# First feed-forward product of five chunks from seven quarter products, with shared buffers

## Chip, cores and metric

The kernel runs on one core of a Trainium2 chip. The metric is device time in microseconds; the median of several runs is compared.

## What is computed

Two layers, each of sliding, dilated attention followed by a dense feed-forward part, both with a layer norm ahead and a residual. The change touches the feed-forward part.

```
B, S, D, F = 1, 2048, 576, 4608      # x [1,2048,576] f32; w1 [576,4608], w2 [4608,576] f32
H, W, dil = 32, 8, 2                 # attention: 32 heads of 18, 8 keys at distance 0,2,..,14

def _A_ref(x, wqkv, wo):             # q,k,v = x@wqkv; softmax over the 8 keys; o @ wo
    ...
def _B_ref(x, w1, w2):
    h = jnp.einsum("bsd,df->bsf", x, w1)
    h = _silu(h)
    return jnp.einsum("bsf,fd->bsd", h, w2)

x = A_x
x = x + _A_ref(_layernorm(x), A_wqkv, A_wo)
x = x + _B_ref(_layernorm(x), B_w1, B_w2)
x = x + _A_ref(_layernorm(x), A_wqkv, A_wo)
x = x + _B_ref(_layernorm(x), B_w1, B_w2)
```

## The kernel before

The 2048 rows are cut into four chunks of 512 (NC = 4, four tiles j of 128 rows), and each of the two layers goes through them, so there are eight stages s = 0 to 7. Every product is made in three passes of f16: an operand is split into a high half and a low half, and high x high, high x low and low x high are summed in PSUM. In a contraction of 576 (four blocks of 128 and one of 64) that is 14 matmuls: `passes` (L333) yields them, the block of 64 holding its high rows and low rows one above the other.

`front(s)` loads the chunk (`load_x`), makes a layer norm whose f16 halves are transposed by DMA on SP's queue (`layer_norm`, `transposed`, L361), makes q, k and v in four units u of eight heads (L564), computes attention on VectorE (L661 to L702), projects with `wo` (`project`, L733) and makes the layer norm for the feed-forward part, whose transposed result XT[s] lies in a buffer `xb`. For the first layer the q, k, v of all chunks are made at the start and lie in DRAM. From s = 4 on, `load_wq` (L510) loads the prepared weights of each unit.

`ffn(s)` works over 36 blocks f of 128 columns of w1. For each: one product z of 14 matmuls with 512 moving columns (L858) into a PSUM bank `z`; ScalarE makes SiLU (L860, tile `hs`) and the high half of h (L862); VectorE makes the low half (L865). Blocks form groups (6 in stage 0, otherwise G1 = 9). For each group and tile j the second product accumulates 6 matmuls per block, 288 columns each (L876), into `acc`, and VectorE adds it to x with the group's scale (L740). In stage 0 the f32 weights are loaded, scaled by powers of two and split (`raw_load`, `raw_split`) and the f16 halves are stored to DRAM (`w1s`, `w2s`); later stages load them from there on SP's queue (L745, L750). The chunk's x goes to DRAM or to the output at the end.

The order of the instructions isn't that of the code. `Plan` collects operations with an engine, a duration, a priority (smaller goes first) and the tiles they read and write; `Plan.order` plays them through, engine by engine, gives each buffer a slot when its first operation starts, and issues the operations in the order so found. So each engine's order, SP's and POOL's DMA queues included, is fixed ahead by these durations. Priorities are tied to the stage: `front(s)` has s - 1, the products of `ffn(s)` s + 0.5, and its loads, ScalarE and VectorE work s - 0.5. A buffer `tag` has its own slots: 2 banks of PSUM for `z`, 2 for `misc` (q, k, v and small sums), 2 x 2 for `acc`; in SBUF for instance 1 `xa` and 2 `xb` (transposed inputs), 2 `wq`, 2 `kv`, 6 `w1`, 11 `w2`, 10 `h`, 3 `hs`.

Of the kernel before, what the change touches and what calls it, by code (L numbers as in the profile page):

```python
# [16 lines left out]
P = 128  # L17
D = 576
# [16 lines left out]
G1 = 9  # L35
LNS = 1024.0
# [14 lines left out]
class Plan:  # L51
# [10 lines left out]
    def slots(self, tag, tiles, turns):  # L62

        self.tags[tag] = tiles
        self.turns[tag] = 0 if turns else None
        self.named[tag] = 0
# [35 lines left out]
    def order(self):  # L102
        free = {t: list(range(len(x))) for t, x in self.tags.items()}
# [63 lines left out]
        while done < len(self.ops):  # L167
# [9 lines left out]
            while events and events[0][0] <= now:  # L177
                _, _, b = heapq.heappop(events)
                free[b.tag].append(b.slot)
            for e in engines:  # L180
# [7 lines left out]
                while ready[e]:  # L188
# [5 lines left out]
                    if all(len(free[t]) - want.get(t, 0) >= c for t, c in n.items()) and all(  # L194
                            self.turns[b.tag] in (None, b.turn) for b in need):
                        o = x[2]
                        break
# [7 lines left out]
                for b in o.bufs:  # L205
                    if b.slot is None:
                        b.slot = free[b.tag].pop(0)
# [24 lines left out]
def sliding_attention_silu_ffn(ctx: ExitStack, tc: tile.TileContext, x, wqkv, wo, w1, w2, out):  # L232
# [17 lines left out]

    tag("x", 8, [P, D], F32)
    tag("xa", 1, [P, 9, TB], F16)
    tag("xb", 2, [P, 9, TB], F16)
    tag("wq", 2, [P, 10, 3 * UC], F16)
    tag("kv", 2, [P, NI, 2, UC], F32)
    tag("qt", 2, [P, NJ, UC], F32)
    tag("o", 1, [P, NJ, D], F32)
    tag("lg", 1, [P, NJ, W, UH], F32)
    tag("pe", 2, [P, NJ, W, UH], F32)
    tag("pr", 1, [P, 2, W, UC], F32)  # L260
    tag("mx", 2, [P, NJ, UH], F32, turns=False)
    tag("y", 2, [P, D], F32, turns=False)
# [3 lines left out]
    tag("w1", 6, [P, 10, P], F16)  # L266
    tag("w2", 11, [P, 2, D], F16)
    tag("h", 10, [P, 2, TB], F16)
    tag("hs", 3, [P, TB], F32)
# [3 lines left out]
    tag("z", 2, [P, TB], F32, ps)  # L273
    tag("acc", 2, [P, 2, 512], F32, ps, turns=False)
    tag("misc", 2, [P, 512], F32, ps, turns=False)
# [3 lines left out]
    w2s = [tc.dram_tile([P, 2 * D], F16, name=f"w2s{f}") for f in range(NFT)]  # L279
    wqs = [tc.dram_tile([P, 30 * UC], F16, name=f"wqs{u}") for u in range(NU)]  # L280
# [35 lines left out]
    shs = [cp.tile([P, NFT], F32, name=f"sh{i}") for i in range(2)]  # L316
    d2s = [cp.tile([P, NFT], F32, name=f"d2{i}") for i in range(2)]
# [30 lines left out]
    def transposed(src, dst, key, j, prio, on_pe=False):  # L348


        if on_pe:
# [6 lines left out]
            op("PE", 0.8, turn, [(src, 0), (src, 1)], [m], prio)  # L358
# [8 lines left out]
    gate = []  # L367
    marks = []

    def layer_norm(xs, prio, into, on_act, on_pe=False):  # L370

        st, mv, nt, xT = Buf("st"), Buf("mv"), Buf("nt"), Buf(into)

# [42 lines left out]
        op("DVE", 2.6, newton, [(st, j) for j in range(NJ)] + [(mv, j) for j in range(NJ) if on_act < 2], [nt], prio)  # L416
        for j in range(NJ):
# [18 lines left out]
            else:  # L436
                op("DVE", 0.6, norm, [xs[j], (mv, j), nt], [y, (xT, "hold")], prio)
# [8 lines left out]
    class Unit:  # L446
# [6 lines left out]

        def __call__(self, k):
            if self.kind == "h":
                return T(self.bufs[k % 5])[:, k // 5, 0:QR]
            return T(self.bufs[0])[:, k, 0:QR]

    def raw_wq(u):

        rs = [Buf("h" if u < 2 else "w2") for _ in range(5)]
# [36 lines left out]
    def store_wq(u, w, m):  # L498
        def store():
# [4 lines left out]
            else:  # L504
                nc.gpsimd.dma_start(wqs[u].rearrange("p (k c) -> p k c", c=QR), T(w.bufs[0])[:, :, 0:QR])
        op("POOL", 2.8 if w.kind == "h" else 0.6, store, w.keys, [("wqs", u)], -0.6, nbytes=P * 20 * QR, after=marks[m:m + 1])

    def load_wq(u, prio):
        w = Unit("wq")
        op("SP", 0.4, lambda: nc.sync.dma_start(fl(T(w.bufs[0])), wqs[u]), [("wqs", u)], w.keys, prio, nbytes=P * 20 * QR)  # L510
        return w
# [83 lines left out]
    def attention(s, xT, wq, more=None):  # L595
# [4 lines left out]
        for u in range(NU):  # L600
# [10 lines left out]
            else:  # L611
                w = wq(u)
                if blk == 0:
# [3 lines left out]
                    op("POOL", 1.6, clear, [], [(kv, "edge")], pr_)  # L617
                else:
# [5 lines left out]
                    op("SP", 0.8, edge, [("eds", lay, par, u)], [(kv, "edge")], pr_, nbytes=20000)  # L624
                for j in range(NJ):
                    m = Buf("misc")

                    def evac(j=j, m=m, u=u, kv=kv, qt=qt):
# [5 lines left out]
                       [(xT, j)] + w.keys, [m], pr_)  # L634
# [52 lines left out]
            for j in range(0, NJ, 2):  # L687
# [15 lines left out]
                op("DVE", 2.63, tree, [], [(pr, 0), (pr, 1), (o, j, u), (o, j + 1, u)], pr_)  # L703
# [51 lines left out]
    def raw_load(f, prio):  # L755
# [15 lines left out]
        op("POOL", 0.6, lambda: nc.gpsimd.dma_start(fl(T(b).bitcast(F32)), w2[f * P:(f + 1) * P, :]), [], [b], prio,  # L771
           nbytes=P * 5 * D, after=late)

    def raw_split(f0, prio):
# [9 lines left out]
        def rb(f):  # L784
            return fl(T(raws[f][1]).bitcast(F32))
# [32 lines left out]
    def group_scale(i, g, n):  # L818

        sl = slice(g * n, (g + 1) * n)  # L820
        sh, d2 = shs[i], d2s[i]
# [6 lines left out]
        op("DVE", 0.7, fn, [("s12", f) for f in range(g * n, (g + 1) * n)], [("sh", i, g), ("cg", g)], -0.5)  # L828

    def ffn(s, xT, xs):  # L830
        raw = s == 0
        n, i = (G0, 0) if raw else (G1, 1)
        pp, pd = s + 0.5, s - 0.5
        lay, c = divmod(s, NC)
        for g in range(NFT // n):
            hb, wbs = [], []
            if raw:
# [5 lines left out]
                group_scale(0, g, n)  # L843
            for f in range(g * n, (g + 1) * n):
# [127 lines left out]
```

## Time and profile before

| | |
|---|---|
| Time, median of 3 runs | 2243.82 us (2238.85 to 2246.42) |
| Span of the profiled execution | 2240.2 us (its own time is not listed apart) |
| TensorE (PE) busy | 2181.8 us, 97% |
| VectorE (DVE) busy | 1396.7 us, 62% |
| ScalarE (ACT) busy | 740.3 us, 33% |
| GpSimd (POOL) busy | 201.4 us, 9% |
| First product L858 | 4032 matmuls, 887.4 us |
| Second product L876 | 6912 matmuls, 855.1 us |
| DMA | 334.54 MB, mean 149 GB/s |

PE is TensorE's matmuls and PEld its weight loads, which overlap them; SPq is the queue from which SP issues DMAs. The listed length of one matmul runs from its issue to its modelled end, so the rate is read from a run of matmuls: length divided by count. In a list of groups the numbers behind the bar are busy us and mean ns of one, then idle us ahead of it and what ended that. The clock is a share of TensorE's full clock; the DMA share is the mean busy share of the core's 16 DMA engines.

### The profile page before, as it was taken

What the parts mean: (1) busy time and instruction counts of PE and PEld (TensorE: products, weight loads), DVE (VectorE), ACT (ScalarE), POOL (GpSimd) and SP (SyncE); (2) the same over time, 40 slices, a digit from 0 to 9 for tenths busy, and PEclk for the clock granted to TensorE, in tenths of its full rate; (3) what the DMA queues carried; (4) which work ended last, traced back from release to release, by engine and by line L of the source; (5) the groups of instructions that cost most, each with busy time, mean ns of one, the idle gap of its engine ahead of it and who ended that gap; (6) DMA issues with size and microseconds to landing.
All of it is one profiled execution on the core that took longest, in us unless ns stands there. A gap on an engine that the chain in (4) does not pass through costs nothing.

```text
span 2240.2 us, 33794 instructions
## 1 busy us (share of the span) xinstructions
PE 2181.8 (97%) x13786; PEld 1349.1 (60%) x13786; DVE 1396.7 (62%) x2074; ACT 740.3 (33%) x1207; POOL 201.4 (9%) x329
## 2 busy tenths in 40 slices
PE   6999998989999999999999999999999999999998
PEld 3446565646766766655666656666666566666665
DVE  8898888979899511259833597346971389511111
ACT  7245675633223122233212232222322223222222
POOL 2123464400001000000000000000000000000000
PEclk9999999999999999999999999999999999999999
DMA  7677676675464433455444454454454643333331
GB/s 199 162 208 257 211 246 202 207 238 175 133 195 149 113 113 104 141 146 171 112 115 153 112 177 117 125 161 123 137 134 119 168 137 119 90 121 121 116 103 40
DMA packets 230148, 334.54 MB, mean 149 GB/s; under 512 B 116696, under 2 KB 136772, under 8 KB 226024
## 3 DMA queue, kind: packets, MB, share of 16 engines
q1 hardware_dynamic: 201024, 225.09, 35.4%
q0 software_dynamic: 19232, 63.86, 8.3%
q10 hardware_dynamic: 9736, 43.42, 6.2%
q8 instruction: 108, 1.77, 0.3%
q14 instruction: 48, 0.39, 0.1%
HBM read 240.08 MB, written 47.03 MB: 128 GB/s over the span
## 4 chain that ended last, share of the span: by engine, by line
issue 44%; PE 42%; DVE 7%; DMA 4%; POOL 1%; ACT 1%; ACTq 0%; POOLq 0%; SPq 0%; DVEq 0%
PE z L858 17%; PE acc L876 17%; PE z L564 3%; PE acc L733 3%; PE misc L564 2%; DVE pr L694 2%; DVE pr L701 1%; DVE lg L665 1%; DVE pr L661 1%; DMA w1s<-w 1%; DMA w<-in_B_w_dram 1%; DMA xb<-yh 0%; DMA w<-w2s 0%; DMA x<-in_A_x_dram 0%; DVE w L804 0%
## 5 line engine op out<-in xcount | busy, mean ns | idle before, releaser
L858 PE MATMUL z<-xb,w 128*128 128x512 f16 x4032 | 887.4, 380 | 19.8 <-ACT hs L860 15.7
L876 PE MATMUL acc<-w,h 128*128 128x288 f16 x6912 | 855.1, 286 | 0.0
L876 PEld LDWEIGHTS <-h 128*128 128x128 f16 x6912 | 676.3, 98 | 177.3
L858 PEld LDWEIGHTS <-w 128*128 128x128 f16 x4032 | 395.5, 98 | 489.4 <-issue 21.9
L860 ACT ACTIVATE hs<-z,d 128x512 f32<-128x512 f32 x288 | 197.4, 685 | 961.3 <-PE z L858 949.9
L865 DVE SCALAR_TENSOR_TENSOR h<-hs,sh,h 128x512 f16<-128x512 f32 x288 | 213.8, 748 | 317.3 <-ACT h L862 317.0
L740 DVE SCALAR_TENSOR_TENSOR x<-acc,d,x 128x576 f32<-128x576 f32 x136 | 110.9, 815 | 321.5 <-PE acc L876 321.3
L661 DVE TENSOR_TENSOR pr<-qt,kv 128x2304 f32<-128x2304 f32 x64 | 163.4, 2553 | 86.6 <-DMA kv<-kv 42.7
L862 ACT ACTIVATE h<-hs,sh 128x512 f16<-128x512 f32 x288 | 207.2, 721 | 9.0
L564 PEld LDWEIGHTS <-xa 128*128 128x128 f16 x1344 | 132.1, 99 | 117.0 <-issue 6.0
L564 PE MATMUL misc<-wq,xa 128*128 128x432 f16 x1008 | 189.4, 349 | 0.7 <-ACT qt L632 0.7
L694 DVE TENSOR_TENSOR pr<-kv,pe 128x1152 f32<-128x1152 f32 x128 | 169.4, 1352 | 1.3
L665 DVE TENSOR_REDUCE lg<-pr 128x128 f32<-128x2304 f32 x64 | 163.2, 2550 | 1.3
L701 DVE TENSOR_TENSOR pr<-pr 128x1152 f32<-128x1152 f32 (+1 forms) x128 | 135.3, 1057 | 3.5
L733 PE MATMUL acc<-wo,oT 128*128 128x288 f16 x896 | 114.5, 289 | 2.9 <-ACT oT L359 2.9
L733 PEld LDWEIGHTS <-oT 128*128 128x128 f16 x896 | 88.3, 99 | 28.7 <-ACT oT L359 3.0
L891 POOL DMA_DIRECT2D out_dram<-x x16 | 8.7, 544 | 910.3 <-DVE x L740 910.3
L630 ACT ACTIVATE kv<-misc,du 128x288 f32<-128x288 f32 x80 | 39.9, 499 | 142.2 <-PE misc L564 73.3
L564 PEld LDWEIGHTS <-xb 128*128 128x128 f16 x448 | 44.8, 100 | 49.1 <-issue 7.7
L684 ACT ACTIVATE pe<-lg 128x256 f32<-128x256 f32 x32 | 13.3, 415 | 167.8 <-DVE lg L675 160.5
L383 DVE BATCH_NORM_STATS2 st<-x 128x6 f32<-128x288 f32 x128 | 51.9, 448 | 10.3 <-DMA x<-xd 6.5
L564 PE MATMUL z<-wq,xb 128*128 128x432 f16 x224 | 43.3, 355 | 5.1 <-DMA xb<-yh 5.1
(118 smaller groups left out, 1094.5 us busy)
## 6 DMA issues: line engine op xcount, KB each, us to landing
w<-w1s SPq DMA_DIRECT2D x252, 320.0 KB
w<-w2s SPq DMA_DIRECT2D x252, 288.0 KB
kv<-kd ACTq DMA_DIRECT2D x12, 1584.0 KB
wq<-wqs SPq DMA_DIRECT2D x17, 1080.0 KB
w1s<-w POOLq DMA_DIRECT2D x36, 320.0 KB, 4.2
w<-in_B_w_dram POOLq DMA_DIRECT2D x36, 288.0 KB, 4.4
w2s<-w POOLq DMA_DIRECT2D x36, 288.0 KB, 4.3
kv<-kv ACTq DMA_DIRECT2D x20, 504.0 KB
```

What stands on the lines that cost most here:

```text
L564: nc.tensor.matmul(T(m)[:, :3 * UC], a, b, start=n == 0, stop=n == len(pl) - 1)
L661: nc.vector.tensor_tensor(T(pr), T(qt)[:, j:j + 2, None, :].to_broadcast([P, 2, W, UC]), win(T(kv), j, 2), op=ALU.mult)
L665: nc.vector.tensor_reduce(T(lg)[:, j:j + 2].rearrange("p a w h -> p (a w h)"), T(pr).rearrange("p a w (h d) -> p (a w h) d", d=DH), axis=A ...
L694: nc.vector.tensor_tensor(T(pr)[:, a].rearrange("p w (h d) -> p w h d", d=DH), v, T(pe)[:, j + a, :, :, None].to_broadcast([P, W, UH, DH]) ...
L701: nc.vector.tensor_tensor(t[:, :, 0:h, :], t[:, :, 0:h, :], t[:, :, h:2 * h, :], op=ALU.add)
L733: nc.tensor.matmul(T(acc)[:, h, 0:288], a, b[:, h * 288:(h + 1) * 288], start=n == 0, stop=n == len(pl) - 1)
L740: nc.vector.scalar_tensor_tensor(t, T(acc)[:, :, 0:288], d, t, op0=ALU.mult, op1=ALU.add)
L858: nc.tensor.matmul(T(z), v, u, start=m == 0, stop=m == len(pl) - 1)
L860: op("ACT", 0.7, lambda z=z, hs=hs, f=f: nc.scalar.activation(T(hs), T(z), AF.Silu, scale=d1[:, f:f + 1]), [z, ("s12", f)], [hs], pd, tabl ...
L862: op("ACT", 0.72, lambda hs=hs, h=h, f=f: nc.scalar.activation(T(h)[:, 0, :], T(hs), AF.Copy, scale=shs[i][:, f:f + 1]), [hs, ("sh", i, g) ...
L865: op("DVE", 0.75, lambda hs=hs, h=h, f=f: nc.vector.scalar_tensor_tensor(T(h)[:, 1, :], T(hs), shs[i][:, f:f + 1], T(h)[:, 0, :], op0=ALU. ...
L876: nc.tensor.matmul(T(acc)[:, h, 0:288], T(hb[q])[:, a, j * P:(j + 1) * P], T(wbs[q][0])[:, w, h * 288:(h + 1) * 288], start=q == 0 and m = ...
```

## The change

**Seven products.** In stages 3 to 7 (SF = 3) two blocks f, a pair p, are made together. The tokens are cut into halves of 256 (HT), the contraction into halves of 288 (HD), the pair into its two blocks: a 2 x 2 by 2 x 2 product. It is made by a scheme with seven products of sums and differences in place of eight. Each product is 7 matmuls with 256 moving columns (three blocks high x high, the third with 96 rows that also hold one crossed part, two low x high and two high x low). Sums that the scheme needs after the products are made partly by accumulating in a PSUM bank that has already been read, partly by ScalarE copies (`keep`) and VectorE additions (`add`).

**Prepared operands.** The layer norm of these stages (`into == "xt"`) makes seven sums of quarters per tile pair, their halves, and 70 transposed blocks per chunk (35 per pass, four DMA transposes for each of two passes) in place of 36 in four. The sums of w1's quarters are made once by `prepare`, 54 pieces (18 pairs times three row blocks): load from w1 by POOL's queue, four subtractions and the low half on VectorE, the high half on ScalarE, and a store to `wts` in DRAM. They have priority 1.2 and may start when stage 0 has all scales. The first 24 use buffer `pw`, the others take turns through `pw`, `pk` and `po`. `load_wt` then loads a pair's 35 blocks into four `w1` slots.

**Groups and buffers.** Groups have 6 blocks in all stages; in stages 3 to 7 the second product is issued one block at a time (STEP) with a priority 0.2 behind the first (LATE). Slots are now w1 8, w2 10, h 8, hs 4, y 1. `Plan` learns of slots that share memory: `xl` (q, k, v input of stages 4 to 7), `x0` to `x2`, the two `xt`, one of the two `wq` and `pw` overlap in one piece of SBUF; `pk` and `po` lie in `kv`, `o` and `pr`, and so do the layer norm's `ys` and `yS`; `zz` covers the four banks of `z` and `misc`. The layer norm, `load_wq` and the edge of keys of stages 4 to 7 wait for the transposes of the stage before, and `load_wq` also for the last four pieces of `prepare`. In the set-up the raw wqkv units change between `h` and `w2` buffers.

```diff
-G1 = 9
-LNS = 1024.0
+G1 = 6
+NP = NFT // 2
+HT = TB // 2
+HD = D // 2
+SF = 3
+PREP = 1.2
+STEP = 1
+LATE = 0.2
+EARLY = 24
+LNS = 512.0
...
+    shared("rb", 3 * XW + QW, [
+        ("wq", [("ra", 0, QW), (3 * XW, 3 * XW + QW)], cut(10), True),
+        ("xa", [(XW * i, XW * (i + 1)) for i in range(3)], cut(9), True),
+        ("xl", [(0, XW), (35 * HT, 35 * HT + XW)], cut(9), True),
...
+        ("xt", [(0, 35 * HT), (35 * HT, 70 * HT)], cut(35), True),
+        ("pw", [("ra", 0, 30 * P), (3 * XW, 3 * XW + 30 * P), (XW, XW + 30 * P)], lambda v: v, True)])
...
+    for t, at, turns in (("z", (0, 1), True), ("misc", (2, 3), False), ("zz", (0, 1, 2, 3), False)):
...
+        op("POOL", 1.2 if k < 2 else 2.4, load, [], [(r, 0)], prio, nbytes=P * 4 * P * 6, after=after)
...
+            nc.vector.tensor_tensor(v[:, 4], v[:, 7], v[:, 0], op=ALU.subtract)
+            nc.vector.tensor_tensor(v[:, 3], v[:, 5], v[:, 7], op=ALU.subtract)
+            nc.vector.tensor_tensor(v[:, 2], v[:, 5], v[:, 4], op=ALU.subtract)
+            nc.vector.tensor_tensor(v[:, 6], v[:, 1], v[:, 2], op=ALU.subtract)
...
+            d = wts[p].rearrange("p (a b c) -> p a b c", a=7, b=5)
+            nc.gpsimd.dma_start(d[:, :, k, :], cut_(0))
+            if k < 2:
+                nc.gpsimd.dma_start(d[:, :, 3 + k, :], cut_(1))
...
+        def product(z, c, m, first):
+            def mm():
+                pl = [(k, k) for k in range(3)] + [(k + 3, k) for k in range(2)] + [(k, k + 3) for k in range(2)]
+                for n, (i, j) in enumerate(pl):
+                    q = 96 if i == j == 2 else P
+                    nc.tensor.matmul(T(z)[:, 0:HT], T(w[m // 2])[0:q, m % 2 * 5 + j, :], T(xT)[0:q, 5 * c + i, :],
+                                     start=first and n == 0, stop=n == len(pl) - 1, skip_group_check=True)
+            op("PE", 0.78, mm, [(xT, 0), (xT, 1), w[m // 2]], [z], pp)
+
+        def keep(z, t, s, k):
+            op("ACT", 0.42, lambda: nc.scalar.activation(T(t)[:, s], T(z)[:, 0:HT], AF.Copy), [z], [(t, k)], pd - 0.2)
+
+        def add(z, t, s, k):
+            op("DVE", 0.43, lambda: nc.vector.tensor_tensor(T(t)[:, s], T(z)[:, 0:HT], T(t)[:, s], op=ALU.add),
+               [z], [(t, k)], pd - 0.2)
...
+        product(Y, 0, 0, True)
+        product(X, 1, 1, True)
+        keep(Y, b, lo, 0)
+        product(Y, 4, 2, False)
+        add(X, b, lo, 0)
+        product(V, 5, 3, True)
+        keep(Y, b, hi, 1)
+        product(Y, 3, 4, False)
+        keep(Y, a, hi, 1)
+        product(Y, 6, 5, False)
+        add(V, a, hi, 1)
+        product(V, 2, 6, False)
+        add(V, b, hi, 1)
+        silu(a, lo, [0], 0.42, Y)
+        silu(a, hi, [1], 0.42)
+        silu(b, slice(0, TB), [0, 1], 0.7)
...
-                step = n if n < 6 else 3
+                step = 3 if s < SF else STEP
...
+        if s == SF:
+            for i in range(3 * NP):
+                t = ("pw", "pk", "po")[(i + i // 3) % 3 if i >= EARLY else 0]
+                prepare(i // 3, i % 3, t, PREP, scaled + {"pw": [], "pk": read[-1:], "po": turned[-2:]}[t])
         ffn(s, XT[s], X[s])
```

More of the change, by code (lines that the diff above doesn't have):

```diff
@@ L102, in order, with spare, hold, fits @@
     def order(self):
-        free = {t: list(range(len(x))) for t, x in self.tags.items()}
+        alias, where = {}, {}
+        for t, us in self.units.items():
+            for i, u in enumerate(us):
+                for x in u:
+                    where.setdefault(x, []).append((t, i))
+        for t, us in self.units.items():
+            for i, u in enumerate(us):
+                alias[t, i] = sorted({k for x in u for k in where[x]})
+        kept = dict.fromkeys(alias, 0)
+        left_at = dict.fromkeys(alias, 0)
+        def spare(t):
+            return [i for i in range(len(self.units[t])) if not kept[t, i]]
+        def hold(t, i, by):
+            for k in alias[t, i]:
+                kept[k] += by
+        def fits(n, want):
+            taken = []
+            ok = True
+            for t, c in n.items():
+                left = spare(t)
+                if len(left) - want.get(t, 0) < c:
+                    ok = False
+                    break
+                if len(n) > 1:
+                    for i in left[:c]:
+                        hold(t, i, 1)
+                        taken.append((t, i))
+            for t, i in taken:
+                hold(t, i, -1)
+            return ok
         engines = sorted({o.eng for o in self.ops})
@@ L178, in order @@
                 _, _, b = heapq.heappop(events)
-                free[b.tag].append(b.slot)
+                hold(b.tag, b.slot, -1)
+                for k in alias[b.tag, b.slot]:
+                    left_at[k] = seq
             for e in engines:
@@ L193, in order @@
                         n[b.tag] = n.get(b.tag, 0) + 1
-                    if all(len(free[t]) - want.get(t, 0) >= c for t, c in n.items()) and all(
-                            self.turns[b.tag] in (None, b.turn) for b in need):
+                    if fits(n, want) and all(self.turns[b.tag] in (None, b.turn) for b in need):
                         o = x[2]
@@ L367, in sliding_attention_silu_ffn, with layer_norm @@
     gate = []
+    turned, scaled, read = [], [], []
     marks = []
-    def layer_norm(xs, prio, into, on_act, on_pe=False):
+    def layer_norm(xs, prio, into, on_act, on_pe=False, late=()):
         st, mv, nt, xT = Buf("st"), Buf("mv"), Buf("nt"), Buf(into)
+        view = lambda: T(xT)
         def total(j, i):
@@ L436, in layer_norm @@
             else:
-                op("DVE", 0.6, norm, [xs[j], (mv, j), nt], [y, (xT, "hold")], prio)
+                op("DVE", 0.6, norm, [xs[j], (mv, j), nt], [y, (xT, "hold")], prio,
+                   after=late)
                 o = op("DVE", 1.2, halves, [y], [(yh, 0), (yh, 1)], prio)
@@ new lines, in load_wt, with load, halves @@
+    def load_wt(p, prio):
+        ws = [Buf("w1") for _ in range(4)]
+        for i, w in enumerate(ws):
+            n = 10 if i < 3 else 5
+            def load(i=i, w=w, n=n):
+                nc.sync.dma_start(fl(T(w))[:, 0:n * P], wts[p][:, 10 * i * P:(10 * i + n) * P])
+            op("SP", 0.5, load, [("wts", p, k) for k in range(3)], [w], prio, nbytes=P * 2 * n * P)
+        return ws
+    def halves(f, hs, h, key, pd):
+        op("ACT", 0.72, lambda: nc.scalar.activation(T(h)[:, 0, :], T(hs), AF.Copy, scale=sh[:, f:f + 1]),
+           [(hs, 0), (hs, 1), key], [(h, 0)], pd)
+        op("DVE", 0.75, lambda: nc.vector.scalar_tensor_tensor(
+            T(h)[:, 1, :], T(hs), sh[:, f:f + 1], T(h)[:, 0, :], op0=ALU.mult, op1=ALU.subtract),
+           [(hs, 0), (hs, 1), (h, 0), key], [(h, 1)], pd)
```

217 lines of the change are left out of this document (165 added, 52 removed).

## The prediction

> **What bounds the kernel now.** I read the page first (busy shares and slices), then busy time by stage, then the chain of waits.
>
> ```profile
> PE 2181.8 (97%) x13786; PEld 1349.1 (60%) x13786; DVE 1396.7 (62%) x2074; ACT 740.3 (33%) x1207; POOL 201.4 (9%) x329
> PE   6999998989999999999999999999999999999998
> DVE  8898888979899511259833597346971389511111
> ...
> 0.00:488.00 488.00, 437.45 (x2670) 261.07 (x2671) 420.51 (x740) 278.90 (x514) 167.10 (x277) 0.98 0.69 217
> 488.00:716.00 228.00, 226.45 (x1462) 143.56 (x1462) 206.30 (x235) 72.16 (x94) 4.02 (x6) 0.99 0.50 159
> 716.00:944.00 228.00, 228.00 (x1480) 144.63 (x1479) 71.63 (x126) 50.70 (x72) 3.94 (x6) 1.00 0.40 120
> 944.00:1213.00 269.00, 269.00 (x1705) 166.64 (x1704) 166.09 (x234) 72.08 (x114) 11.52 (x17) 1.00 0.49 138
> 1751.70:2021.00 269.30, 269.30 (x1706) 166.74 (x1705) 162.21 (x224) 71.85 (x114) 2.19 (x5) 1.00 0.46 128
> ```
>
> The windows are my stages: set-up with chunk 0, then chunk 1, chunk 2, chunk 3 (with the attention of chunk 4), and the sixth chunk; their columns are PE, PEld, DVE, ACT and POOL busy, then clock, DMA share, GB/s. From 500 us on TensorE never idles and its clock is 1.00. So each chunk after the first lasts as long as its matmuls, and the change, which touches chunks 3 to 7, is priced on TensorE. VectorE is the other thing to watch: 206 of 228 us in chunk 1, but 72 of 228 in chunk 2.
>
> **The gain: the products.** From the chain in order of time (start, length, what, count), and a short stretch with small matmuls:
>
> ```profile
> 660.38 27.20 PE z L858 x126
> 687.58 26.46 PE acc L876 x216
> 966.55 25.55 PE misc L564 x140
> ...
> 218.59 1.17 PE L357 MATMUL acc<-ident,yh 128*128 128x128 f16 x18
> ...
> L876 PEld LDWEIGHTS <-h 128*128 128x128 f16 x6912 | 676.3, 98 | 177.3
> L357 PE MATMUL acc<-ident,yh x108: 217/219/314, 13.0 to 222.6; 128*128 128x128 f16 x108
> ```
>
> A matmul of 512 columns takes 27.20/126 = 0.2159 us, of 432 columns 25.55/140 = 0.1825, of 288 columns 26.46/216 = 0.1225. The line through these is 0.4167 ns a column and 2.5 ns fixed, so 256 columns cost 0.1092 us (estimate). Every matmul has its own weight load, listed at 98 ns; could that be a floor? The 18 transposes of 128 columns, each with its own load, take 1.17 us to the end of the last; less its 0.219 us, 0.95/17 = 0.056 us each. No floor as high as 0.109.
>
> For two column blocks f the kernel now issues 2 x 14 matmuls of 512: 6.04 us. The change issues 7 products x 7 matmuls of 256: 49 x 0.1092 = 5.35 us (the matmuls on 96 rows stream the same columns). That saves 0.69 us a pair, 18 pairs and 5 chunks: 62.2 us. The second product (L876) keeps its 864 matmuls a chunk.
>
> The Trainium skill, "TensorE: Matmul & The Clock Gate", section "Back-to-back issue gap", speaks against this: in a stream of weight loads and matmuls it gives about 81 ns a matmul at 128 columns and 131 at 512, so about 98 at 256 by a straight line (an estimate from that page). By that, a pair would go from 28 x 0.131 = 3.7 us to 49 x 0.098 = 4.8 us, and the kernel would lose some 100 us. The trace disagrees at both ends (0.056 and 0.2159 us), and its measured line decides.
>
> **What it adds on ScalarE and VectorE.** The nearest rows:
>
> ```profile
> L860 ACT ACTIVATE hs<-z,d 128x512 f32<-128x512 f32 x288 | 197.4, 685 | 961.3 <-PE z L858 949.9 <-DMA kv<-kv 3.2 <-DVE lg L665 3.1
> L630 ACT ACTIVATE kv<-misc,du 128x288 f32<-128x288 f32 x80 | 39.9, 499 | 142.2 <-PE misc L564 73.3 <-DVE pr L694 56.1 <-issue 9.1
> L632 ACT ACTIVATE qt<-misc,du 128x144 f32<-128x144 f32 x80 | 29.9, 374 | 0.0
> L684 ACT ACTIVATE pe<-lg 128x256 f32<-128x256 f32 x32 | 13.3, 415 | 167.8 <-DVE lg L675 160.5 <-DMA kv<-kv 7.2
> L675 DVE TENSOR_TENSOR lg<-lg,mx 128x256 f32<-128x256 f32 x32 | 13.6, 425 | 1.1
> L740 DVE SCALAR_TENSOR_TENSOR x<-acc,d,x 128x576 f32<-128x576 f32 x136 | 110.9, 815 | 321.5 <-PE acc L876 321.3
> L804 DVE SCALAR_TENSOR_TENSOR w<-w,s,w 128x640 f16<-128x640 f32 x36 | 31.7, 880 | 8.4 <-ACT w L802 8.4
> L802 ACT ACTIVATE w<-w,s 128x640 f16<-128x640 f32 x36 | 29.5, 819 | 21.1 <-DMA w1s<-w 10.7 <-PE z L858 9.6 <-DVE s L330 0.4
> L661 DVE TENSOR_TENSOR pr<-qt,kv 128x2304 f32<-128x2304 f32 x64 | 163.4, 2553 | 86.6 <-DMA kv<-kv 42.7 <-ACT kv L630 21.7 <-ACT qt L632 21.2
> L702 DVE TENSOR_TENSOR o<-pr 128x288 f32<-128x288 f32 x64 | 29.3, 458 | 2.6
> ```
>
> Per pair ScalarE gets three copies out of PSUM of 256 columns (0.47 us each, between L632 and L630) and its SiLU in three pieces (0.47, 0.42, 0.69) in place of two of 0.69: +1.6 us, 29 us a chunk, on an engine that is busy 72 of 269. VectorE gets three adds of 256 (0.425): 23 us a chunk; 24 in place of 16 adds into x (groups of 6): 6.5 us; the wider layer norm about 3 us. So 166 + 32 = 198 busy us in a chunk of 257. Both hide beside TensorE as long as order allows.
>
> The weight preparation is 54 pieces, from the end of chunk 0 on. Each: four subtractions of 128 columns (0.29 us, by the slope from L675 to L702) and one low half of 896 columns (1.16, slope of L740 and L804) on VectorE, 2.33 us; 1.03 us on ScalarE. That is 126 us of VectorE, 56 of ScalarE. VectorE had 456 - 278 = 178 us idle in chunks 1 and 2; groups of 6 take 13 and the norm 3. So 126 of 162 us fits before chunk 3, mostly in chunk 2. If that cover is gone, the rest falls into chunk 3 (59 us idle there).
>
> **What is late next: the front of chunk 4.** Its weight loads (L510) are made to wait for the last pieces and for the transposes of chunk 3; on SP's queue feed-forward weight loads stand behind them.
>
> ```profile
> 979.36 7.99 SPq L510 DMA_DIRECT2D wq<-wqs  x2
> ...
> 1135.95 7.71 SPq L361 DMA_TRANSPOSE xb<-yh  x4
> ...
> 1940.60 9.98 SPq L361 DMA_TRANSPOSE xb<-yh  x4
> ...
> L361 SPq DMA_TRANSPOSE xb<-yh x36: 1242/1300/4112, 30.7 to 1949.3; - x36
> ```
>
> Today the front of chunk 4 ends about 1146 and is needed at 1213: 67 us spare (the sixth chunk's: 1951 against 2021). After: 12 less from the shorter chunk, about 25 more VectorE work ahead of it, and four more transposes of 1.3 us each with their landing, some 8 us. Spare 20 us, provided the pieces end by about 979, where those loads go today. I take 5 us of stall at this boundary, between 0 (ends in time) and 59 (all of chunk 3's idle VectorE time used up by pieces ahead of it).
>
> **DMA.** Two windows calibrate: one with weight loads alone, one with transposes in small packets.
>
> ```profile
> DMA packets 3004, 6.48 MB, mean 116 GB/s; under 512 B 332, under 2 KB 332, under 8 KB 3002
> q1 hardware_dynamic: 3002, 6.45, 36.9%
> ...
> DMA packets 4881, 1.52 MB, mean 102 GB/s; under 512 B 4752, under 2 KB 4752, under 8 KB 4880
> q1 hardware_dynamic: 4880, 1.51, 49.3%
> ```
>
> The first (56 us, 2072 to 2128) moves 6.45 MB at 36.9%, so 312 GB/s when full; the second (15 us, 1940 to 1955) 1.51 MB at 49.3%: 204 GB/s. A pair's weights grow from 20 to 35 blocks of 32 KB, 0.66 to 1.15 MB: 8.8 MB a chunk, 28 us of full DMA; the 70 transposed blocks in place of the window's 36 some 7 us more. The share of chunks 3 to 6 rises from 0.49 to about 0.65; I cost it at nothing, since two pairs of weight buffers cover 11 us a pair. The prepared weights go out as 256-byte pieces, 18 x 1.15 = 20.6 MB: at 204 GB/s 101 us, and 54 x 0.26 = 14.2 MB of f32 quarters come in, 45 us: 146 us on top of a half-idle DMA over the 350 us from about 600 on. POOL issues these 234 transfers and is all but idle then (4 us per chunk). The Trainium skill, "DMA: Bandwidth & Descriptors", section "Specifications", says that pieces under 512 bytes lose line rate to read-modify-write; the second window agrees in direction (204 against 312 GB/s).
>
> **Waits within a pair.** Seven products share three banks; Y is read twice, and product 4, 3 and 6 each wait for a read; V's second product waits for a VectorE add. Between them the planner puts pieces of the second product (0.73 us, now one block at a time). The planner counts 0.42 us for the copies that I put at 0.47, so I take 2 x 0.05 = 0.1 us a pair, 9 us for 90 pairs. Below: nothing, as TensorE shows none now. Above: 3.4 us for a pair in an attention stretch (rival A).
>
> **Nothing on the path:** the smaller h, y and w2 buffer counts meet a first stage held by VectorE (420 of 488 us); I allow 8 us either way there.
>
> **Sum.** 2240.2 span - 62.2 + 9 + 5 = 2192. The page gives no time of its own for the profiled execution; the span lies 3.6 us under the median of 2243.8, so 2195.6; I say 2195.
>
> **Rivals.**
> A, slower: VectorE holds the products. While attention runs, its order is filled with operations of 2.55 us (L661). An add that arrives behind one waits 1.28 us on average, then takes 0.43; two per pair sit before a product (the bank of X, the second half of V): 3.4 us if nothing covers. About 110 us of VectorE-saturated time per chunk 3 to 6 is 8 pairs, 32 in all: 109 us in place of the 9 of the sum: 2195 - 9 + 109 = 2295. It decides once the mean wait over all 90 pairs passes 0.69 us. Against it: 24 free pieces of the second product per 21 products. Chance 0.13.
>
> B, part of the gain lost to the preparation: small stores and the gate on chunk 4's front run late, 20 to 40 us of stall near 1200: 2210 to 2237. For it: spare of only 20 us by my count; against: TensorE needs a pair's weights only every 14 us from 944 on. Chance 0.12.
>
> C, no change: a floor per matmul between the rows, at most the 0.1225 us of 288 columns: 882 x 0.1225 = 108.0 us a chunk against 108.8: 4 us gained, 2240. The transposes speak against it. Chance 0.05.
>
> D, slower: a weight load's 98 ns stands in series with each matmul. A pair then pays 21 loads more, 378 a chunk, 37 us; over five chunks 185 us less the gain: 2366. The run of 126 matmuls in 27.20 us has no room for a load in series. Chance 0.01. (It is the direction of the issue-gap section of the Trainium skill's "TensorE: Matmul & The Clock Gate" above.)
>
> A long stall would also cost clock:
>
> ```profile
> 489.55 17.30 PE L858 MATMUL z<-xb,w 128*128 128x512 f16 x70 [6.76 <-ACT hs L860]
> 480.00:490.00 10.00, 3.24 (x15) 0.84 1.01 395
> 490.00:500.00 10.00, 10.00 (x40) 0.82 0.40 140
> ```
>
> After 6.76 us idle 70 matmuls took 17.3 us where 15.1 would do, so a stall of that size costs a third more.
>
> **Chances.** Forecast, gain mostly kept (2176 to 2210): 0.66, and 0.03 for better (a shorter first stage). With B (0.12), C (0.05), A (0.13) and D (0.01). A difference of 0.3%, 6.7 us, is about what a measurement of this kernel can tell from none: faster 0.80 (the far end of B touches the bound), same 0.06, slower 0.14. The range 2172 to 2236 holds forecast and B and leaves out A, C and D.
>
> **What would show it.** Right: matmuls of 256 columns at about 0.109 us in a run of them; TensorE time of a first product down from 108.8 to 96.3 us per chunk; chunks 4 to 6 lasting 257 us; VectorE near 90% from 488 to 944. Wrong: TensorE idle before the product lines released by VectorE adds (A), idle around 1200 or waiting for the prepared weights (B), or a run of 256-column matmuls above 0.12 us (C).

## The result, and the profile after

The changed kernel takes 2211.54 us (median of 4 runs, 2204.07 to 2215.92) against 2245.12 us (2238.85 to 2246.79) for the kernel before on the same chip: ratio 0.9864, interval 0.9835 to 0.9892. It is 34 us faster, where 2195 had been forecast: 49 us. The profiled execution took 2212.85 us and its span is 2211.0 us. In the line numbers of the changed kernel the first product is L1118 (512 columns) and L1045 (256 columns, chunks 3 to 7), the second L1131, the copies out of PSUM L1050, the adds L1053, the transposes of a chunk's input L439 and those of its operand for the feed-forward part L534.

Busy shares on the page, then the stages in the same windows as before:

```profile
PE 2128.8 (96%) x15676; PEld 1532.1 (69%) x15676; DVE 1647.7 (75%) x2658; ACT 934.2 (42%) x1649; POOL 384.1 (17%) x563
```

```profile
488.00:716.00 228.00, 228.00 (x1480) 144.65 (x1478) 219.76 (x324) 86.53 (x108) 71.16 (x90) 1.00 0.75 218
716.00:944.00 228.00, 224.00 (x1439) 141.28 (x1438) 147.06 (x280) 86.24 (x108) 100.04 (x127) 0.99 0.77 199
944.00:1213.00 269.00, 262.23 (x2115) 206.20 (x2113) 202.77 (x324) 104.26 (x196) 26.13 (x35) 1.00 0.62 183
1751.70:2021.00 269.30, 268.62 (x2182) 212.65 (x2181) 194.39 (x297) 107.63 (x208) 2.16 (x4) 1.00 0.63 181
```

TensorE still sets the time, but it now idles: 4 us in the second window, 7 in the third. The first two windows also show where VectorE did not go: it is full in chunk 1 (219.8 of 228), yet has 81 us free in chunk 2, in which 29 of the 54 pieces are made.

From the order in time on TensorE (start, length, what, count): the first product of chunk 3 before the change, then after it that of chunks 3 to 7 and a pair's 49 matmuls with the line behind them.

```profile
942.22 24.34 PE L858 MATMUL z<-xb,w 128*128 128x512 f16 x112
```

```profile
947.77 2.47 PE L1045 MATMUL z<-rb,w 128*128 128x256 f16 x21
...
1218.58 3.35 PE L1045 MATMUL z<-rb,w 128*128 128x256 f16 x16 [8.68 <-DMA rb<-o]
1223.23 2.03 PE L1045 MATMUL z<-rb,w 96*128 96x256 f16 x17 [1.30 <-DMA rb<-o]
...
1482.84 3.35 PE L1045 MATMUL z<-rb,w 128*128 128x256 f16 x29
...
1742.95 3.24 PE L1045 MATMUL z<-rb,w 128*128 128x256 f16 x28
...
2003.54 3.68 PE L1045 MATMUL z<-rb,w 128*128 128x256 f16 x32
...
2099.38 5.54 PE L1045 MATMUL z<-rb,w 128*128 128x256 f16 x49
2104.76 0.90 PE L1131 MATMUL acc<-w,h 128*128 128x288 f16 x6
```

The 49 matmuls take 2104.76 - 2099.38 = 5.38 us, 0.1098 us each. The chunks last 270.8 (chunk 3, of which 8.7 are the stall at its end), 264.3, 260.1, 260.6 and 207.5 us (of chunk 7, 14 matmuls went ahead, at 1990); before, from first product to first product, they took 269.2 each and the last 221.1 us. Chunk 3 starts at 947.8, 5.6 us later than before (942.2). So the gain of the products is there from chunk 4 on, and two things took part of it away: a late start of chunk 3 and the wait for the operand of chunk 4.

All waits of TensorE from chunk 3 to the end:

```profile
PE z L1045 <- DMA rb<-o: 10.0, 2, 8.7
PE z L1045 <- DVE hs L1053: 3.6, 3, 1.5
PE z L1045 <- ACT hs L1050: 2.4, 5, 0.5
PE acc L1131 <- DVE x L866: 2.0, 4, 0.9
```

The first row is the boundary at 1213; the others, within pairs and groups, come to 9 us with three small ones that aren't shown (0.8, 0.4 and 0.2). VectorE's adds (rival A) hold the products for 3.6 us in all.

### The profile page after: what moved, and what is told of

It is laid out like the page before. It is cut to its first block, busy times and chain, and to the rows that moved or that the text cites. A ratio compares the mean times of both kernels' runs of the same rounds, so it can differ in the third digit from the quotient of the medians.

```text
span 2211.0 us, 39442 instructions
## 1 busy us (share of the span) xinstructions
PE 2128.8 (96%) x15676; PEld 1532.1 (69%) x15676; DVE 1647.7 (75%) x2658; ACT 934.2 (42%) x1649; POOL 384.1 (17%) x563
## 4 chain that ended last, share of the span: by engine, by line
PE 42%; issue 41%; DVE 7%; DMA 6%; ACT 2%; POOL 1%; SPq 1%; ACTq 0%; POOLq 0%; DVEq 0%
PE acc L1131 16%; PE z L1118 11%; PE z L690 6%; PE z L1045 6%; PE acc L859 2%; DMA oT<-yh 2%; DMA w<-in_B_w_dram 1%; DVE pr L820 1%; DMA rb<-yh 1%; DVE pr L827 1%; DVE pr L787 1%; DVE lg L791 1%; DMA qd<-hs 1%; DVE x L866 0%; DVE st L463 0%
## 5 line engine op out<-in xcount | busy, mean ns | idle before, releaser
L1131 PE MATMUL acc<-w,h 128*128 128x288 f16 x6912 | 884.7, 286 | 2.5 <-DVE x L866 2.4
L1131 PEld LDWEIGHTS <-h 128*128 128x128 f16 x6912 | 675.9, 98 | 175.7 <-issue 3.4
L1045 PE MATMUL z<-rb,w 128*128 128x256 f16 (+1 forms) x4410 | 523.7, 273 | 17.4 <-DMA rb<-o 10.0
L1045 PEld LDWEIGHTS <-w 128*128 128x128 f16 (+1 forms) x4410 | 429.8, 97 | 85.5 <-issue 16.9
L1118 PE MATMUL z<-rb,w 128*128 128x512 f16 x1512 | 336.0, 381 | 11.7 <-ACT hs L1120 5.1
L690 PEld LDWEIGHTS <-rb 128*128 128x128 f16 x1792 | 177.4, 99 | 169.7 <-issue 18.4
L1118 PEld LDWEIGHTS <-w 128*128 128x128 f16 x1512 | 148.5, 99 | 186.4 <-issue 5.0
L1050 ACT ACTIVATE hs<-z 128x256 f32<-128x256 f32 x270 | 98.7, 379 | 336.1 <-PE z L1045 304.2
L1053 DVE TENSOR_TENSOR hs<-z,hs 128x256 f32<-128x256 f32 x270 | 109.7, 418 | 148.9 <-PE z L1045 85.7
L690 PE MATMUL z<-ra,rb 128*128 128x432 f16 x952 | 186.8, 353 | 13.1 <-DMA rb<-yh 11.0
L1120 ACT ACTIVATE hs<-z,d 128x512 f32<-128x512 f32 x108 | 73.9, 685 | 187.2 <-PE z L1118 174.2
L1057 ACT ACTIVATE hs<-hs,dt 128x256 f32<-128x256 f32 (+1 forms) x180 | 109.9, 612 | 94.1 <-DVE hs L1053 94.0
```

The lines of the kernel that those rows point to most:

```text
L690: nc.tensor.matmul(T(m)[:, :3 * UC], a, b, start=n == 0, stop=n == len(pl) - 1)
L1045: nc.tensor.matmul(T(z)[:, 0:HT], T(w[m // 2])[0:q, m % 2 * 5 + j, :], T(xT)[0:q, 5 * c + i, :], start=first and n == 0, stop=n == len(pl) ...
L1118: nc.tensor.matmul(T(z), v, u, start=m == 0, stop=m == len(pl) - 1)
L1131: nc.tensor.matmul(T(acc)[:, h, 0:288], T(hb[q])[:, a, j * P:(j + 1) * P], T(wbs[q][0])[:, w, h * 288:(h + 1) * 288], start=q == 0 and m = ...
```

## Where the 34 us come from

Two runs divide the change. The first keeps the new buffers and groups of 6 and makes no chunk with seven products:

```diff
-SF = 3
+SF = 8
...
-"xt" if s >= SF else f"x{s}"
+"xt" if s >= SF else ("x0", "x1", "x2", "x1", "x2", "x1", "x2", "x1")[s]
```

> All of the change but the seven products: shared buffers, groups of 6, other buffer counts; the first product of all chunks is made as before and nothing is prepared. Theory P: no better and no worse than before, 2244 plus or minus 6. Theory B: 10 to 20 us slower than before, 2254 to 2264, with idle TensorE time at the chunk boundaries.

Measured: 2237.21 us (2232.58 to 2240.73, 10 runs), ratio 0.9967 [0.9953, 0.9982], span 2234.3. The buffers and groups alone are worth some 8 us, slightly more than either expectation had. In that run the first product of chunk 1, of which 28 matmuls are done by then, goes on at 484.27 without idle time ahead of it:

```profile
484.27 12.25 PE L1118 MATMUL z<-rb,w 128*128 128x512 f16 x56
```

The 6.76 us wait that the kernel before has at 489.55 is gone, and chunk 3 starts at 934.9 instead of 942.2.

The second halves the preparation: 27 pieces in place of 54, and the pairs 9 to 17 load the weights of pairs 0 to 8. That changes the computation, but not the number or size of the other operations.

```diff
-wts[p][:, 10 * i * P:(10 * i + n) * P]
+wts[p % 9][:, 10 * i * P:(10 * i + n) * P]
...
-            for i in range(3 * NP):
+            for i in range(3 * NP // 2):
```

> Only the weights of pairs 0 to 8 are prepared (27 pieces in place of 54); pairs 9 to 17 load the weights of pairs 0 to 8, so the computation is changed there; all matmuls, loads and layer norms stay. Theory P (the preparation makes the front of chunk 4 late and takes TensorE's cover): the front's first attention operation moves from 1024 us back to about 990, the 10 us of TensorE idle before chunk 4 and the 4 us around 780 go, and the time falls from 2211 to about 2196. Theory B (shared buffers, groups of 6 and the wider layer norm make the fronts late): the time stays at 2208 to 2213.

Measured: 2190.88 us (2187.36 to 2202.26), ratio 0.9769 [0.9731, 0.9807], span 2185.6. VectorE's first attention product of chunk 4, and the first product of chunk 4 on TensorE:

```profile
990.71 2.56 DVE L787 TENSOR_TENSOR pr<-qt,kv 128x2304 f32<-128x2304 f32 x1 [15.88 <-DMA kv<-kv]
```

```profile
1197.33 5.54 PE L1045 MATMUL z<-rb,w 128*128 128x256 f16 x49
```

Attention starts where it did before (990.14), chunk 4 starts without a stall, chunk 3 at 937.9. So the 34 us are, rounded: 8 from buffers and groups, 46 from seven products (2237.2 to 2190.9), and 21 lost to the second half of the preparation (2190.9 to 2211.5). The four times of this run lie 15 us apart, so the last two are known to some 5 us. By the spans of the profiled executions the loss is 25.4 us: chunk 3 starts 9.9 us later, chunk 3 lasts 11.3 us longer, the rest is spread behind. The first 27 pieces cost chunks 1 and 2 nothing that shows: chunk 3 starts 3.0 us later with them than in the run without any, but chunk 1's first product is already as far behind (it begins at 481.2, where the run without any has 28 matmuls, 6.0 us, done by 484.3), so the 3.0 us come from the set-up.

## Why the preparation was late

The front of chunk 4 in the changed kernel, in order of time on POOL, SP's queue and VectorE; the last line is VectorE's first attention product of chunk 4 in the kernel before:

```profile
977.73 1.02 POOL L1011 DMA_DIRECT2D wts<-o  x1 [0.29 <-DVE o L1003]
```

```profile
978.95 0.44 SPq L635 DMA_DIRECT2D ra<-wqs  x1
...
981.15 4.95 SPq L439 DMA_TRANSPOSE rb<-yh  x1
...
997.16 2.95 SPq L439 DMA_TRANSPOSE rb<-yh  x2
...
1207.22 7.59 SPq L534 DMA_TRANSPOSE rb<-kv  x4
1215.04 5.71 SPq L534 DMA_TRANSPOSE rb<-o  x4
```

```profile
1024.09 2.56 DVE L787 TENSOR_TENSOR pr<-qt,kv 128x2304 f32<-128x2304 f32 x1 [17.05 <-DMA kv<-kv]
```

```profile
990.14 2.56 DVE L661 TENSOR_TENSOR pr<-qt,kv 128x2304 f32<-128x2304 f32 x1 [21.23 <-DMA kv<-kv]
```

The last piece is stored at 978 and the weights of chunk 4 load at 979, as before. But the input's transposes now come behind them (981 to 1000), and the first attention product starts at 1024, 34 us later than before. Three edits asked what sets the pace of the pieces.

**The gate.** The loads of chunk 4's weights and the clearing of its keys no longer wait for the last four pieces:

```diff
-            after=turned[-2:] + preps[-4:])
+            after=turned[-2:])
...
-op("POOL", 1.6, clear, [], [(kv, "edge")], pr_, after=turned[-2:] + preps[-4:])
+op("POOL", 1.6, clear, [], [(kv, "edge")], pr_, after=turned[-2:])
```

> The q, k, v weight loads and the clearing of the key buffer of stages 4 to 7 no longer wait for the last four pieces of the preparation, only for the layer norm's transposes; buffers still decide. Theory gate: the front of chunk 4 gets its weights about 20 us earlier and its first attention operation moves from 1024 to about 1000, the stall before chunk 4 shrinks to 3 us or less, 2199 to 2205. Rival: the front is held by pieces still in the key, o and pr buffers and ahead of it in VectorE's order, so nothing moves by more than 5 us: 2207 to 2214.

Measured: 2208.46 us (2199.51 to 2217.72), ratio 0.9846 [0.9819, 0.9872]. The first attention product is at 1023.4 all the same, the pieces end later (994), and chunk 4 waits 5.0 us:

```profile
PE z L1045 <- DMA rb<-o: 5.0, 4, 3.5
```

The gate alone is not the cause: without it the front is as late. The five times lie 18 us apart, so the 3 us of gain are not clear of noise; and since the pieces also moved by 16 us, what the gate would cost at their old pace isn't shown.

**The small stores.** Each row of a piece is stored in runs of 1792 bytes in place of 256. The blocks are then fetched in another order, which changes the computation.

```diff
-d = wts[p].rearrange("p (a b c) -> p a b c", a=7, b=5)
+d = wts[p].rearrange("p (b a c) -> p a b c", a=7, b=5)
```

> The prepared weights are laid out in DRAM so that each store writes 1792 consecutive bytes per partition in place of seven pieces of 256; the loads are unchanged and so fetch the blocks in another order, so the products use the wrong blocks. Amounts of data and all instructions stay. Theory P1 (the small stores pace the preparation): the pieces end 30 us or more before 978, chunk 4 starts without a stall, 2193 to 2203. Theory P2 (not the stores but the waiting for the last pieces and VectorE's load make the front of chunk 4 late): pieces end within 15 us of now, 2207 to 2214.

Measured: 2206.8 us (2202.13 to 2208.64), ratio 0.9831 [0.9809, 0.9853]. A store lands in 3.8 to 4.3 us instead of 4.5 to 5.5 (medians by buffer), the pieces end at 972 instead of 978, and the stall stays:

```profile
1214.36 3.41 PE L1045 MATMUL z<-rb,w 128*128 128x256 f16 x16 [9.47 <-DMA rb<-o]
```

The Trainium skill, "DMA: Bandwidth & Descriptors", section "Specifications", sets 512 bytes as the least transfer at line rate; the landing times agree in direction. But the small stores do not pace the pieces: longer ones end them only 6 us sooner.

**The planner's sizes.** The plan takes a piece's load for 393 KB and its stores for 917 KB (the `nbytes` of L989 and L1012); they move 262 and 459 KB (every third piece stores only 229). Told so, and nothing else changed:

```diff
-op("POOL", 1.2 if k < 2 else 2.4, load, [], [(r, 0)], prio, nbytes=P * 4 * P * 6, after=after)
+op("POOL", 1.2 if k < 2 else 2.4, load, [], [(r, 0)], prio, nbytes=P * 4 * P * 4, after=after)
...
-op("POOL", 1.2, store, [(r, 2), (r, 3)], [("wts", p, k)], prio, nbytes=P * 14 * P * 4)
+op("POOL", 1.2, store, [(r, 2), (r, 3)], [("wts", p, k)], prio, nbytes=P * 14 * P * 2)
```

> Only the sizes that the planner is told of a piece's transfers change, to what they move: load 262 KB in place of 393, store 459 KB in place of 918. No operation is added or taken away, only the fixed order of the engines changes. Theory order (the planner's slow transfers space the pieces 9 us apart in VectorE's and POOL's order, while they land after some 5 us): the pieces end 40 us or more before 976, the first attention operation of chunk 4's front comes before 1005, the stall before chunk 4 goes, 2190 to 2200. Rival (the transfers themselves, or VectorE, set the pace): the pieces end within 15 us of now, 2206 to 2216, or more where engines now wait in order for transfers.

The last store of a piece, the first attention product and the first product of chunk 4:

```profile
931.04 0.93 POOL L1011 DMA_DIRECT2D wts<-o  x1 [0.24 <-DVE o L1003]
```

```profile
995.02 2.56 DVE L787 TENSOR_TENSOR pr<-qt,kv 128x2304 f32<-128x2304 f32 x1 [15.92 <-DMA kv<-kv]
```

```profile
1200.92 5.54 PE L1045 MATMUL z<-rb,w 128*128 128x256 f16 x49
```

The pieces end 47 us earlier and attention starts 29 us earlier; TensorE goes into chunk 4 17.7 us earlier than in the changed kernel and without a stall. So it was the plan that spaced the pieces. And yet the time is 2214.42 us (2210.12 to 2218.69), ratio 0.9876 [0.9851, 0.9902]: nothing won.

## Why an earlier preparation did not help

Two more orders put the preparation earlier, by its priority alone and together with the sizes:

```diff
-PREP = 1.2
+PREP = 0.9
```

> The priority of the preparation goes from 1.2 to 0.9, so it comes ahead of the attention of chunk 2 instead of behind it. That attention has some 80 us to spare (the layer norm of chunk 2 was ready at 630 us, needed at 713). Theory P: the pieces end at 920 to 950 instead of 978, the front of chunk 4 is no longer late, 2196 to 2204. Rival: the pieces are paced by their transfers and buffers, not by VectorE's order, and end as late as now; the time stays at 2208 to 2214, or is longer if chunk 2 now waits.

> The true transfer sizes and the preparation's priority at 0.9, ahead of the attention of chunk 2. Theory order: pieces end before 900, no stall before chunk 4, 2188 to 2200. Rival: as with the priority alone (2212), the time won before chunk 4 is lost again later in the chunks' products: 2206 to 2216.

They took 2212.33 us (2210.73 to 2215.69; ratio 0.986 [0.9826, 0.9895]) and 2208.28 us (2205.31 to 2212.14; 0.9848 [0.9825, 0.9872]). In both chunk 4 starts some 15 us earlier, and the end does not move. The run with the true sizes shows where the time goes. Waits of TensorE from chunk 3 on:

```profile
PE z L1045 <- ACT hs L1050: 12.8, 8, 6.2
PE z L1045 <- DMA rb<-o: 3.3, 2, 1.9
```

The longest of them, in order of time:

```profile
1273.45 11.65 ACTq L768 DMA_DIRECT2D kv<-kv  x4
...
1285.15 0.38 ACT L1050 ACTIVATE hs<-z 128x256 f32<-128x256 f32 x1 [11.08 <-DMA kv<-kv]
...
1285.58 2.72 PE L1045 MATMUL z<-rb,w 128*128 128x256 f16 x12 [6.18 <-ACT hs L1050]
```

ScalarE issues four copies within the key buffer (L768; they fill its halo, keys that a partition needs from another one). Three go out at once; the fourth goes out at 1284.29, after a wait for a transfer of these keys, while the DMA share is 0.86 to 1.07 (stretches of 2 us). Behind it in ScalarE's order stands the copy that frees TensorE's bank. The same happens once more near 1870 (3.3 us). At the end of the span 15.8 of the 17.7 us are gone: some 9.5 by these two waits, 3.3 by those at chunk 6's operand (the second row), the rest wasn't traced.

Two runs move these four issues to GpSimd, one of them with the true sizes:

```diff
-nc.scalar.dma_start(t[p0 + d:p0 + d + n, i:i + m], t[p0:p0 + n, 11 - m:11])
+nc.gpsimd.dma_start(t[p0 + d:p0 + d + n, i:i + m], t[p0:p0 + n, 11 - m:11])
...
-op("ACT", 3.2, halo, own, [(kv, "halo")], pr_ - 0.2, nbytes=P * 14 * UC * 4)
+op("POOL", 3.2, halo, own, [(kv, "halo")], pr_ - 0.2, nbytes=P * 14 * UC * 4)
```

> The changed kernel with the planner told the true transfer sizes of the pieces (as in e10_real_sizes) and, in addition, the four copies within the key buffer that fill its halo (L768) issued by GpSimd in place of ScalarE. In the run with the sizes alone ScalarE held the copies out of PSUM (L1050) twice behind the fourth of these issues, 11.1 and 7.4 us, and TensorE idled 6.2 and 3.3 us for it. Theory H (the time won before chunk 4 is given back because a transfer issue blocks ScalarE's order): both waits go, TensorE waits less than 5 us on L1050 from 1200 us on, and the time falls by about 9 us against the sizes alone, to about 2203 (2196 to 2208). Theory R (the order has no slack: whatever wait is removed, the next operation of a front is late): the L1050 waits are replaced by others, for instance on transposes (rb from o) or on the halo itself at L787, and the time stays at 2208 to 2216.

Measured: 2217.93 us (2208.51 to 2220.31), ratio 0.988 [0.9855, 0.9905]. Theory H missed the time by 10 us and more, but the waits went as it said: on L1050 2.4 us are left. TensorE's waits from chunk 3 on, then those of the first 488 us, then the first product of chunk 3:

```profile
PE z L1045 <- ACT hs L1050: 2.4, 5, 0.5
PE z L1045 <- DMA w<-wts: 2.3, 2, 1.5
```

```profile
PE acc L859 <- DMA oT<-yh: 9.9, 2, 6.0
```

```profile
967.75 2.47 PE L1045 MATMUL z<-rb,w 128*128 128x256 f16 x21
```

From chunk 3 to the end it takes 2218.5 - 967.75 = 1250.7 us; the changed kernel takes 1263.2, the run with the sizes alone 1267.2 (from 941.9), the run with half the pieces 1247.7. So behind the start of chunk 3 both losses are closed, the stall at chunk 4 and the held copies of ScalarE. But the edit moves the copies of the set-up too, TensorE there waits, among others, for the transposed attention output (9.9 us, where the changed kernel waits 1.7), and chunk 3 starts 26 us later than with the sizes alone. The start of the one with the rest of the other would be a span of 941.9 + 1250.7 = 2193 us, an estimate: moving the copies of chunks 4 to 7 alone wasn't tried.

> The changed kernel with only the four halo copies (L768) moved from ScalarE to GpSimd. The preparation keeps its pace, so by both theories chunk 4 still waits 6 to 12 us for its transposes near 1210. Theory H: in the changed kernel L768 holds ScalarE only briefly and TensorE waits 1.5 us on L1050 in chunks 4 to 7, so there is little to win: 2206 to 2212. Theory R: 2208 to 2216, and both theories come apart in the other run, not here; this one shows what the move alone costs or brings.

Without the sizes the move makes it worse than either theory said: 2233.71 us (2228.29 to 2238.59), ratio 0.9957 [0.9939, 0.9974]. The pieces end at 993, and chunk 4 waits twice as long:

```profile
1238.82 3.60 PE L1045 MATMUL z<-rb,w 128*128 128x256 f16 x16 [19.71 <-DMA rb<-o]
```

Three runs show how little room the fronts have. In the first the last second products of chunks 2 to 6 go behind the first products of the next chunk, as cover for the wait at 1213:

```diff
-pp + (LATE if s >= SF else 0))
+pp + (LATE if s >= SF else 0) + (1.0 if SF - 1 <= s < 7 and g == NFT // n - 1 else 0))
```

> In chunks 2 to 6 the second product of the last group gets a priority behind the first products of the next chunk, so it can fill TensorE's waits at the start of that chunk (2.4 us at chunk 3's start, about 4 after chunk 4's, 0.6 at each of the next two). Theory W (with pieces of the second product at hand the waits within a pair vanish): 4 to 8 us less, 2203 to 2208. Rival: x is finished later, the next front starts later, and as much is lost: 2209 to 2220.

Measured: 2235.8 us (2228.49 to 2242.57), ratio 0.9966 [0.9948, 0.9984]. The stall at 1213 stays and a larger one comes at chunk 6, since x is finished later and the next layer norm with it (in chunk 6's front its transposes come 11 us later, its attention 29):

```profile
PE z L1045 <- DMA rb<-o: 30.1, 4, 19.7
```

In the changed kernel the last transposes of the operands of chunks 5 to 7 are issued 9, 13 and 5 us before the first product that reads them; before, it was 66 to 69 us.

The other two make chunks 4 to 7 alone with seven products, so that the preparation has a chunk more; in the second the pieces are issued sooner, those in `po` wait for the same reads as those in `pk`, and the gate is gone. In both, the operands of chunks 0 to 3 take turns in x0 to x2.

```diff
-SF = 3
+SF = 4
```

> The seven products begin with chunk 4 instead of chunk 3 (four chunks), the preparation is as now. One chunk's gain of 12.4 us is given up. Theory P: the pieces have a chunk more of time and no front is late, so the stall of about 13 us and what chunk 3's start loses go too: 2208 plus or minus 5, no worse than five chunks. Theory B: the loss stays and the gain is smaller, 2220 to 2226.

```diff
-SF = 3
+SF = 4
...
-            after=turned[-2:] + preps[-4:])
+            after=turned[-2:])
...
-        if s == SF:
+        if s == SF - 1:
```

> Seven products from chunk 4 on (four chunks); the pieces are prepared from the same point on as with five chunks, and only the buffers, not a wait, tie the front of chunk 4 to them. From the run with shared buffers alone (2237) and the 9.8 us that a chunk gained with half the pieces: 2237 - 4 x 9.8 = 2198 plus or minus 5 if nothing waits for the pieces. If the pieces still delay the front of chunk 4, whose norm is now the wide one, the chunk 4 start is late as with five chunks: 2208 to 2215.

Both are slower than before: 2275.52 us (ratio 1.0137 [1.0106, 1.0168]) and 2270.04 us (1.012 [1.0102, 1.0139]). One chunk less should cost some 10 us against the changed kernel; it cost about 60. The pieces now take their turns in key and product buffers beside a chunk's attention and last until 1323 and 1152; that this is the cause is read from the order in time, no run separates it. The first run's waits at chunk 5's projection and operand, and the second's at the projection near 1233:

```profile
1502.24 16.70 PE L859 MATMUL acc<-wo,oT 128*128 128x288 f16 x112 [29.14 <-DMA oT<-yh]
...
1541.06 3.57 PE L1045 MATMUL z<-rb,w 128*128 128x256 f16 x16 [22.11 <-DMA rb<-o]
```

```profile
1233.40 16.00 PE L859 MATMUL acc<-wo,oT 128*128 128x288 f16 x112 [37.35 <-DVE nt L489]
```

## Why the prediction was right, and where it was off

The time of 2211.5 us lies in the range of 2172 to 2236, but at the foot of rival B's 2210 to 2237 and above the forecast's 2176 to 2210. By spans the forecast was 2240.2 - 62.2 + 9 + 5 = 2192; the runs give 2240.2 - 5.9 (buffers and groups) - 48.7 (seven products with half the pieces) + 25.4 (the other half) = 2211.0. The gain came from the mechanism that was forecast; the preparation took more of it than forecast.

- **The rate** held: 0.1098 us a matmul against 0.1092 from the line through three other widths, so 96.8 us of first product a chunk where 96.3 was put. Rivals C and D are out; a pair's 49 weight loads, listed at 98 ns each (4.8 us), fit beside its 5.38 us of products. The Trainium skill, "TensorE: Matmul & The Clock Gate", section "Back-to-back issue gap", has a sustained figure of 131 ns at 512 columns and a formula for one matmul by itself, N/2.4 + 2.5 ns, which gives 109 at 256 (an estimate from that page). The sustained stream here follows the formula.
- **The products** were forecast to gain 62.2 - 9 = 53 us. The run with half the pieces is 51.7 us faster from chunk 3's first product to its end than the run without seven products (1299.4 against 1247.7). Chunks 5 and 6 last 260 us where 257 was put. That the waits come to 9 us, as in the sum, is luck: the sum had 0.1 us in every pair, because a copy (470 ns) would take longer than the plan's 420; a copy takes 379, an add 418 where 425 was put, and the waits lie in a few places, 7 us of them before first products, the others before second products and a projection. With half the pieces all of them come to 6 us.

```profile
L1053 DVE TENSOR_TENSOR hs<-z,hs 128x256 f32<-128x256 f32 x270 | 109.7, 418 | 148.9 <-PE z L1045 85.7 <-ACT hs L1050 55.9 <-ACT qt L758 6.5
L1050 ACT ACTIVATE hs<-z 128x256 f32<-128x256 f32 x270 | 98.7, 379 | 336.1 <-PE z L1045 304.2 <-issue 18.2 <-DVE h L1027 8.1
```

- **The step that failed is "What is late next: the front of chunk 4", 5 us, together with the DMA at nothing.** They measured 25 us of span (21 by medians) in place of 5. The text made the spare depend on the pieces ending by 979, and they did (978). But it let only the weight loads wait for them and took the input's transposes and the keys from the order before; these came 30 us later. The last attention operation of chunk 4's front, before and after:

```profile
1102.36 0.46 DVE L702 TENSOR_TENSOR o<-pr 128x288 f32<-128x288 f32 x1
```

```profile
1160.92 0.46 DVE L828 TENSOR_TENSOR o<-pr 128x288 f32<-128x288 f32 x1
```

  So attention starts 34 us later and lasts 25 us longer, the latter as forecast. From its end to the operand's first transpose (1135.95 before, 1207.22 after) it takes 46 us in place of 33, 8 of these 13 in the wider layer norm, for which 3 had been put. The eight transposes themselves add only some 1.5 us until the first product, where 8 had been put; and chunk 4 could have begun at 1209.9, 1.5 us earlier than before (1211.4) and not 12, since chunk 3 started late. Together 34 + 25 + 13 + 3 is 75 us against 66 of spare: the stall of 9 us. That is rival B's mechanism, with half of its size at that place.
- **The start of chunk 3** was not a term at all. In chunk 2, where the DMA engines are full (share 0.99), TensorE waits before the attention's projection, the second time for transposes; waits, and the window around the second (clock, DMA share, GB/s are the last three):

```profile
780.68 7.02 PE L859 MATMUL acc<-wo,oT 128*128 128x288 f16 x56 [1.35 <-DVE x L866]
...
794.76 5.52 PE L859 MATMUL acc<-wo,oT 128*128 128x288 f16 x30 [2.65 <-DMA oT<-yh]
```

```profile
780.00:800.00 20.00, 16.67 (x122) 12.52 (x122) 9.73 (x18) 1.21 (x2) 13.60 (x18) 0.91 0.99 170
```

  Chunk 1's first product, in the changed kernel and with half the pieces:

```profile
485.08 18.29 PE L1118 MATMUL z<-rb,w 128*128 128x512 f16 x84
```

```profile
481.18 18.29 PE L1118 MATMUL z<-rb,w 128*128 128x512 f16 x84
```

  Of the 9.9 us by which chunk 3 starts earlier with half the pieces, 3.9 are there already at chunk 1, from the set-up; why, no run shows. The other 6.0 arise in chunk 2: the 4.0 us of idle time in the two rows above, and some 1.8 us by the clock, 0.91 over 20 us.
- **The first stage** was put at "8 us either way". The buffers and groups gained 8, by spans 5.9; without the 8 the time would have been about 2219.
- **VectorE** near 90% from 488 to 944 was wrong for chunk 2 (147 of 228): the pieces were spaced by the plan, not by the engine.
- **Small readings:** the slope from L740 and L804 gives 1.14 us for the low half of a piece, not 1.16, and 1.14 was measured.

## What to carry to other kernels

In a static order, price a step that is moved by everything that the order ties to it: what bounded the new work was neither its engine nor its bytes, but its place among the operations that had to follow. Sizes told to the planner are part of the kernel, and correcting one shows the next mismatch; follow a saved stall to the end of the trace before counting it. A transfer issued from an engine that also frees PSUM banks can hold TensorE when that issue waits (6.2 us here).

## What the hardware showed

A matmul of 256 columns with its own weight load runs at 0.1098 us, on the same line as 288, 432 and 512 columns. Behind the 8.68 us stall 16 such matmuls took 3.35 us at a granted clock of 0.55 (1218 to 1222; 1.00 in the 4 us behind), where 1.92 would do by the rate with the tail of the last one: the stall costs some 1.4 us beyond itself, a sixth, where the prediction put a third for such a stall. The Trainium skill, "TensorE: Matmul & The Clock Gate", Part 1, says that the clock falls to half after an idle window of about 3.4 us; the 0.55 behind 8.68 us agrees. A copy of 128x256 f32 out of PSUM on ScalarE takes 379 ns when its scale is a constant, where 374 ns had been seen for 144 columns and 499 for 288 with a scale read per row. And the fourth of four transfers issued by one engine waited 9.4 us while the first three did not; why the fourth, no run shows.
